# Copies within DRAM from unit 6 on, the gating moved behind a sum, another bank pair: five edits to one attention and MLP kernel

## The chip, the cores and the metric

The kernel runs on one core of one Trainium2 chip. The metric is device time in microseconds (us) of one execution; a kernel's time is the median of several. The profile comes from one profiled execution. The engines are PE (TensorE: matmuls, with PEld for its weight loads), DVE (VectorE), ACT (ScalarE), POOL (GpSimd) and SP (SyncE), which here only issues DMAs.

## The reference

One block of a transformer with modulated layer norms: attention over the last 512 keys of a cache, then a gated MLP, both added to x. All is fp32.

```python
W = min(4096, max(256, Sk // 4))                       # 512 of 2048 keys
q = (x @ wq).reshape(B, Sq, 32, 128)
scores = einsum("bhqd,bhkd->bhqk", q, k) * 128 ** -0.5 # 16 kv heads for 32 heads
o = softmax(scores) @ v
x = x + ga * (o @ wo)                                  # h = layernorm(x) * (1 + ca) + sa went in
gate = h @ W_gate; up = h @ W_up                       # h = layernorm(x) * (1 + cb) + sb
x = x + gb * (relu(gate) * up) @ W_down
```

x has 2048 rows of 576, the MLP is 4608 wide.

## The kernel before

**Precision.** Every matmul operand is split into hi + lo, two numbers of PE's rounded fp32 type, and a product is hi\*hi + lo\*hi + hi\*lo. ACT casts to hi, POOL subtracts to get lo.

**Attention** runs in 128 units u, each one head against 512 queries. A unit issues on PE: 12 matmuls of scores (L454 to L456), 14 of the next unit's q (L382), 2 that spread the maxima (qm, L482), 12 of the last unit's o (pv, L556 to L558, in two halves `pv_half`), and two pieces of 12 that multiply o by wo and go into acc (L583). Most units subtract the maximum on DVE (L529); the first four and the last let PE subtract it (L525, from mr). POOL makes the lo parts (L538) and part of the sums (L547).

**Steps.** A table of steps (time, function) puts everything else between these: time t = 10 u + k means unit u, slot k. On PE, DVE, ACT and POOL the written order is the order that runs. SP is not under that rule: the framework orders its DMAs by what they wait for and when they come up, so a step's time is only one input to its place there. SP issues one DMA after another, in its order; a load whose buffer isn't free holds up all behind it.

**Loads.** wq (L188, rwA), kv (L202, rkv) and wo (L217, roga) come in per head, each into one of two raw buffers, are gated (wo only, L221 on DVE) and split. `wm` (L136) are loads of the modulation, `wa_P` and `wb_P` (L844) those of early MLP weights.

**Copies within DRAM.** wg and wu are laid out anew in DRAM, in `wlay` (and `wlay0` for the first two tiles), by 152 DMAs from SP (`lay_steps`, issued at L1196). 20 of them fill wlay0. 68 are blocks of shape 2 x 128 x 256 (256 KB), and 64 are strips of 8 or 9 x 32 x 128. The MLP's first half and the steps `w_later` (from t = 546) read the result.

**MLP.** 36 steps m, in two halves over the rows; each makes seven products P1, P6, P2, P7, P5, P4, P3 (a Strassen-like scheme, `prod`, L928, gu), in two halves of 7 matmuls. A product's result takes a pair of PSUM banks from the list `free`, two pairs tagged s, and a third pair tagged x that opens when attention's last tiles of the pool psM are done. P2 and P3 go on in the pairs of P1 and P5. Between a product's halves come `sums` (weights of the scheme, DVE, L734, tiles wr and ws), `others` (loads, splits), and one piece of the down projection of m - 1 (`md_piece`): 12 matmuls (L583) into one bank pair, of which there is one, and the sum into acc on DVE (L594). The second product has two such pieces, one before and one behind its second half. Behind the second half, `evac` reads the product (L949 to L953, L975, L978). `mextra` holds functions for a given product; those marked `sums` are the gating of wd (rogb, L221; in the second and the fourth product of an m) and the statistics of the second layer norm (`ln_half`, at the end of m = 1, 3, 5 and 7). After m = 18 wd and the split weights come back from DRAM, without gating.

**Between the two**, steps h0 prepare the MLP's first inputs: `h0_comb` on DVE (L797), `h0_hi` on ACT, `h0_cut` (L817, L819). In the list below H is 1070; the third number is a step's offset.

Of the kernel before, what the change touches and what calls it, by code (L numbers as in the profile page):

```python
# [21 lines left out]
NFT = F // P  # L22
# [11 lines left out]
def kernel(  # L34
# [13 lines left out]
    nc = tc.nc  # L48
# [211 lines left out]
    def flush(q=None):  # L260
        q = pend if q is None else q
        while q:
            q.pop()()
# [143 lines left out]
    NU = HKV * NQB * 2  # L407
# [10 lines left out]
    def unit(u):  # L418
        return UNITS[u]
# [21 lines left out]
    st_, t4, t5, pt, hi_, lo_, bc, rb, rinv, ks_, pvps, done, o, bps = ({} for _ in range(14))  # L441
# [107 lines left out]
    def pv_half(u, h):  # L549
        g, qb, hd = unit(u)  # L550
        if h == 0:
            pvps[u] = psM.tile([P, 512], F32, tag="mm", name=f"pv{u}")
        ps, v, a, b = pvps[u], vs[g], hi_[u, h], lo_[u, h]
        for j in range(2):
            kt = 2 * h + j
            nc.tensor.matmul(ps, v[:, kt, :], a[:, j, :], start=(kt == 0), stop=False)  # L556
            nc.tensor.matmul(ps, v[:, 4 + kt, :], a[:, j, :], start=False, stop=False)  # L557
            nc.tensor.matmul(ps, v[:, kt, :], b[:, j, :], start=False, stop=(kt == 3))  # L558
        if h:
            done[u] = pvps.pop(u)  # L560
# [91 lines left out]
    def order(m):  # L652
        return ("P1", "P6", "P2", "P7", "P5", "P4", "P3")
# [16 lines left out]
    def lay_steps():  # L670
        def tiles(f):
            return [(wlay[f:f + 2, j, :, xx, 0:256], src[f:f + 2, :, 256 * j:256 * j + 256])
                    for xx, src in enumerate((wg, wu)) for j in range(2)]

        def rest(f, g):
            return [(wlay[f:g, j, 32 * r:32 * r + 32, xx, 256:384], src[f:g, 32 * j:32 * j + 32, 512:640])
                    for xx, src in enumerate((wg, wu)) for j in range(2) for r in range(4)]

        def first(s):
            return [(wlay0[:, j, :, xx, 0:256] if w is None else wlay0[:, j, 32 * r:32 * r + 32, xx, 256:384],  # L680
                     a[0:2, :, 256 * j:256 * j + 256] if w is None else a[0:2, 32 * j:32 * j + 32, 512:640])
                    for xx, a in enumerate((wg, wu)) for j in range(2) for w, r in s]

        return (first([(None, 0)] + [(1, r) for r in range(4)]),
                [s for f in range(2, NFT, 2) for s in tiles(f)] +
                [s for f in (2, 10, 19, 28) for s in rest(f, {2: 10, 10: 19, 19: 28, 28: 36}[f])])
# [232 lines left out]
    def prod(m, s, n, xx):  # L919

        hs, w = hop[m // NFP, OPS[s][1]], wop[n]
        ps = pair[m, s][:, xx, :]
        ops = []
        for t in range(2):
            ops += [(w[:, xx, t, :], hs[t]), (w[:, xx, 3 + t, :], hs[t]), (w[:, xx, t, :], hs[3 + t])]
        ops.append((w[0:96, xx, 2, :], hs[2][0:96]))
        for i, (a, c) in enumerate(ops):
            nc.tensor.matmul(ps, a, c, start=s not in ("P2", "P3") and i == 0, stop=i == len(ops) - 1,  # L928
                             skip_group_check=True)
# [27 lines left out]
    npair, px, free, kind = [0], {}, ["s", "s"], {}  # L957
# [71 lines left out]
    def step(name, t, fn, *args):  # L1029
        sched.append((t + PLAN.get(name, 0), len(sched), fn, args))  # L1030
# [161 lines left out]

    step("T.ohi2", e, o_hi, NU - 2)
    step("T.olo2", e, o_lo, NU - 2)
    for i, ab in enumerate(sum(lay_steps(), [])):
        step("lay", 400 + 3.5 * i, lambda ab=ab: nc.sync.dma_start(*ab))  # L1196
    mextra = {}

    def mat(m, s, fn, sums=False):
# [12 lines left out]
    for i in range(4):  # L1212
        m = 2 + 2 * i
# [10 lines left out]
    def sums(m, i):  # L1224

        for k, s in {1: [(0, "S1")], 2: [(0, "S4")], 5: [(1, "S3")], 6: [(1, "S2")]}.get(i, []):
            if 0 < m + k < NFP:
                w_sums(m + k, s)
        for fn in mextra.pop((m, i - 1, True), []):
            fn()  # L1230

    def others(m, i):
        w_prep(7 * m + i + 2)
# [6 lines left out]
    def mlp_slots():  # L1240
        for m in range(NB):
            md = [lambda k=k, qt=qt: md_piece(m - 1, k, qt) for k in range(2) for qt in range(4)] if m else []
            for i, s in enumerate(order(m)):
                flush_stores()
                if s not in ("P2", "P3"):
                    new_pair(m, s)
                else:
                    pair[m, s], kind[m, s] = (x[m, {"P2": "P1", "P3": "P5"}[s]] for x in (pair, kind))
                prod(m, s, 7 * m + i, 0)
                if m or i:  # L1250
                    sums(m, i)
                    others(m, i)
                if m and i:
                    md.pop(0)()
                elif filler and not m:
                    filler.pop(0)()
                prod(m, s, 7 * m + i, 1)
                wop.pop(7 * m + i)
                if m and i < 2:
                    md.pop(0)()  # L1260
                elif filler and not i:
                    filler.pop(0)()
                evac(m, s)
                if s not in ("P1", "P5"):
                    free.append(kind[m, s])
                yield
        for k in range(2):
            for qt in range(4):
                md_piece(NB - 1, k, qt, (psS, "s") if qt % 2 else None)
        flush_stores()  # L1270
        assert not mextra and not filler
# [10 lines left out]
    def open_x():  # L1282
        psM_scope.__exit__(None, None, None)
        px["x"] = ctx.enter_context(tc.tile_pool(name="psX", bufs=1, space=bass.MemoryType.PSUM,
                                                 reuse_waits="tile"))
        free.insert(0, "x")
        filler.extend([lambda q=q: wo_piece(NU - 1, q)() for q in range(4)])


# [19 lines left out]
    for key, t, at_ in [(("l", 0, 0), 2, 96), (("l", 1, 0), 2, 96), (("l", 1, 1), 2, 122), (("l", 0, 1), 2, 122),  # L1309
# [6 lines left out]
        if key[0] == "l":  # L1316
            step("h0.l", H + at_, h0_load, *key[1:], t)
        elif key in H0_COMB:
            step("h0.a", H + at_, h0_comb, *H0_COMB[key], t)
        else:  # L1320
            step("h0.h", H + at_, h0_hi, key, H0_CUT[key], t)
            step("h0.c", H + at_ + (6 if t == 2 else 4 if at_ // 10 % 2 else 6),
                 then(lambda key=key, t=t: h0_cut(key, H0_CUT[key], t, key == "T2")))
# [38 lines left out]
    for u in range(NU):  # L1362
        run(u, 0)
        if u > 1 and u % 2 == 0:
            o_hi(u - 2)
            o_lo(u - 2)
        s_half(u, 0)
        s_half(u, 1)
        max_pre(u)
        if u:  # L1370
            sum_pre(u - 1)
        run(u, 1)
        if u + 1 < NU:
            qproj(u + 1, 0, 14)
        else:
            piece(at[10 * u + 1])
        run(u, 2)
        spread(u)
        max_bc(u)
        if u + 1 < NU:  # L1380
            q_hi(u + 1)
        run(u, 3)
        if 10 * u + 3 in at:
            piece(at[10 * u + 3])
        if u > 1 and u % 2:
            o_hi(u - 2)
            o_lo(u - 2)
        run(u, 4)
        if u:
            pv_half(u - 1, 0)  # L1390
        flush(pend_act)
        exp_half(u, 0)
        flush()
        run(u, 5)
        exp_half(u, 1)
        if u:
            sum_bc(u - 1)
        if u + 1 < NU:
            q_lo(u + 1)
        ksum_op(u, 0)  # L1400
        ksum_op(u, 1)
        run(u, 6)
        if u:
            pv_half(u - 1, 1)
        if 10 * u + 6 in at:
            piece(at[10 * u + 6])
        run(u, 7)
        if u:
            o_mul(u - 1)
        flush()  # L1410
        run(u, 8)
        hi_half(u, 1)
        flush(pend_act)
        lo_half(u, 0)
        lo_half(u, 1)
        run(u, 9)
# [56 lines left out]
```

## Time and profile before

| | |
|---|---|
| median of 3 runs | 3032.86 us (3030.03 to 3036.67) |
| profiled execution, its own time | 3032.14 us |
| its span, first to last instruction | 3030.4 us |
| mean granted clock of PE | 0.985 |
| first matmul of the MLP (L928) | 1704.62 us from the span's start |
| HBM read and written | 278.17 MB, 172.20 MB |

In the views an instruction stands as: line, engine, operation, out<-in, shapes, count. A row of a timeline ends with the idle time ahead of it and what ended that. The chain of waits goes back from the last instruction to what released each one; shares of it are shares of time on the path that set the end. SPq rows are DMA issues on SP; their length is the time of the issue, not of the transfer.

### The profile page before, as it was taken

Reading aid. Unit: us, or ns where it says so; the run is one execution under the profiler, and the core shown is the slowest. Engines: PE = TensorE matmul, PEld = TensorE weight load, DVE = VectorE, ACT = ScalarE, POOL = GpSimd, SP = SyncE. Lnnn points to the kernel's source line nnn. Section 1 sums busy time; section 2 is a strip of 40 time slices with the busy share of each in tenths; the row PEclk is TensorE's granted clock in tenths of the full one; section 3 lists DMA queues with packets and bytes.
Section 4 is the critical chain, followed back from the end, with each engine's and each line's share of the span. In section 5 each row is a group of like instructions: output and inputs, shape, how many; then the busy total and the mean of one; then the engine's idle time right before and its main releaser. Section 6 shows DMA issues by size and latency. Waiting matters only on the chain.

```text
span 3030.4 us, 41167 instructions
## 1 busy us (share of the span) xinstructions
PE 2901.1 (96%) x15406; PEld 2527.0 (83%) x15406; DVE 2116.5 (70%) x2916; ACT 1365.2 (45%) x1869; POOL 1857.3 (61%) x1308
## 2 busy tenths in 40 slices
PE   6799999999978899999999899999999999999999
PEld 4688888888757788888888788888788888888888
DVE  7888888888746788877889666677777544444444
ACT  4467666676545576666656433333323111111110
POOL 5588888888856788876778666667777211111111
PEclk9899999999989999999999999999999999999999
DMA  4011121112222223322233466667666944444543
GB/s 145 21 50 52 50 72 68 66 55 85 102 81 98 90 92 103 129 103 76 77 117 130 133 232 232 251 252 271 254 253 256 347 161 162 162 162 170 177 157 115
DMA packets 167304, 424.75 MB, mean 140 GB/s; under 512 B 15425, under 2 KB 62273, under 8 KB 167105
## 3 DMA queue, kind: packets, MB, share of 16 engines
q1 hardware_dynamic: 131472, 291.58, 29.1%
q10 hardware_dynamic: 35632, 130.53, 10.8%
q8 instruction: 122, 2.00, 0.3%
q14 instruction: 78, 0.63, 0.1%
HBM read 278.17 MB, written 172.20 MB: 149 GB/s over the span
## 4 chain that ended last, share of the span: by engine, by line
PE 83%; DVE 7%; DMA 4%; POOL 2%; issue 2%; ACT 2%; SPq 0%; ACTq 0%; POOLq 0%; DVEq 0%
PE gu L928 25%; PE md L583 14%; PE wo L583 12%; PE qps L382 11%; PE s L455 3%; PE s L456 3%; PE s L454 3%; PE pv L558 3%; PE pv L557 3%; PE pv L556 3%; DVE wr L734 1%; DMA roga<-wo 1%; DMA rkv<-kv 1%; PE qm L482 1%; DVE rogb L221 1%
## 5 line engine op out<-in xcount | busy, mean ns | idle before, releaser
L538 POOL TENSOR_TENSOR lo<-p,hi 128x1024 fp32r<-128x1024 f32 x256 | 610.1, 2404 | 0.9 <-DVE t L474 0.9
L547 POOL TENSOR_TENSOR ks<-ks,p 128x512 f32<-128x512 f32 x256 | 342.6, 1338 | 284.9 <-ACT p L531 218.0
L594 DVE TENSOR_TENSOR acc<-md,acc 128x576 f32<-128x576 f32 x288 | 217.5, 755 | 394.3 <-PE md L583 393.8
L583 PE MATMUL md<-wogb,hhi 128*128 128x288 f32 x2304 | 472.4, 297 | 17.8 <-DVE acc L594 17.8
L583 PEld LDWEIGHTS md<-wogb,hhi 128*128 128x128 f32 x2304 | 384.9, 189 | 46.6 <-DVE acc L594 26.3
L459 DVE TRANSPOSE_TENSOR_REDUCE t<-s 128x32 f32<-128x1024 f32 x256 | 316.5, 1243 | 138.0 <-PE s L456 126.8
L928 PE MATMUL gu<-hop_B,wop 128*128 128x512 f32 (+1 forms) x1512 | 372.5, 393 | 0.0
L583 PE MATMUL md<-wogb,hlo 128*128 128x288 f32 x1152 | 340.9, 296 | 0.0
L382 PE MATMUL qps<-hTa,wA 128*128 128x512 f32 x1288 | 314.8, 396 | 21.5 <-DVE rb L564 11.7
L944 POOL TENSOR_TENSOR hlo<-r,hhi 128x512 fp32r<-128x512 f32 x72 | 94.2, 1309 | 382.9 <-issue 240.9
L583 PE MATMUL wo<-woga,ohi 128*128 128x288 f32 x1472 | 313.3, 306 | 16.1 <-ACT wo L616 14.5
L928 PEld LDWEIGHTS gu<-hop_B,wop 128*128 128x128 f32 (+1 forms) x1512 | 279.7, 189 | 54.6 <-ACT lflh L913 0.4
L928 PE MATMUL gu<-hop_T,wop 128*128 128x512 f32 (+1 forms) x1260 | 313.2, 392 | 3.0 <-DVE rb L564 3.0
L382 PEld LDWEIGHTS qps<-hTa,wA 128*128 128x128 f32 x1288 | 246.4, 192 | 74.7 <-DVE rb L564 12.2
L529 DVE TENSOR_TENSOR p<-s,mb 128x1024 f32<-128x1024 f32 x246 | 290.7, 1219 | 13.0 <-POOL lo L538 8.8
L518 ACT CAST hi<-p 128x1024 fp32r<-128x1024 f32 x256 | 269.0, 1051 | 7.1
L928 PEld LDWEIGHTS gu<-hop_T,wop 128*128 128x128 f32 (+1 forms) x1260 | 231.2, 188 | 46.6 <-DVE rb L564 3.1
L583 PEld LDWEIGHTS wo<-woga,ohi 128*128 128x128 f32 x1472 | 244.4, 193 | 24.9 <-ACT wo L616 15.9
L531 ACT ACTIVATE p<-p 128x1024 f32<-128x1024 f32 x246 | 259.8, 1056 | 8.0 <-DVE p L529 7.9
L943 ACT CAST hhi<-r 128x512 fp32r<-128x512 f32 x72 | 44.7, 621 | 462.0 <-DVE r L953 458.7
L434 ACT ACTIVATE qhi<-qps 128x512 fp32r<-128x512 f32 x128 | 76.5, 597 | 325.8 <-PE qps L382 325.8
L583 PE MATMUL wo<-woga,olo 128*128 128x288 f32 x736 | 220.7, 300 | 0.1
(205 smaller groups left out, 6308.0 us busy)
## 6 DMA issues: line engine op xcount, KB each, us to landing
wop<-wk_P SPq DMA_DIRECT2D x133, 640.0 KB
wk_P<-wop ACTq DMA_DIRECT2D x119, 640.0 KB
wr<-wlay SPq DMA_DIRECT2D x68, 384.0 KB
dk<-wogb ACTq DMA_DIRECT2D x36, 576.0 KB
wogb<-dk SPq DMA_DIRECT2D x36, 576.0 KB
againq<-akq SPq DMA_DIRECT2D x18, 640.0 KB
rogb<-wd SPq DMA_DIRECT2D x36, 288.0 KB
rwA<-wq SPq DMA_DIRECT2D x32, 320.0 KB
```

The lines of the kernel that those rows point to most:

```text
L382: return [lambda i=i, a=a, b=b: nc.tensor.matmul(ps, a, b, start=(i == 0), stop=(i == n - 1)) for i, (a, b) in enumerate(ops)]
L454: nc.tensor.matmul(ps, k[:, kt, :], qhi[u], start=True, stop=False)
L459: nc.vector.tensor_reduce(t4[u][:, 2 * h:2 * h + 2, :].rearrange("p k b -> p (k b)"), t.rearrange("p k (b j) -> p (k b) j", j=32), axis=AX ...
L518: nc.scalar.copy(hi_[u, h], pt[u, h])
L529: nc.vector.tensor_tensor(p, t, bc[u][:, None, :].to_broadcast([P, 2, 512]), op=ALU.subtract)
L531: nc.scalar.activation(p, p, AF.Exp, bias=0.0, scale=1.0)
L538: nc.gpsimd.tensor_sub(lo_[u, h], pt[u, h], hi_[u, h].bitcast(F32))
L547: nc.gpsimd.tensor_tensor(ks_[u], ks_[u], p[:, j, :], op=ALU.add)
L583: nc.tensor.matmul(ps[:, half, :H2], a[:, sl], w[b][:, cs], start=(n == 0 and seed is None), stop=(n == 5), skip_group_check=seed is not None)
L594: nc.vector.tensor_tensor(av, ps[:, :, :H2], av, op=ALU.add)
L928: nc.tensor.matmul(ps, a, c, start=s not in ("P2", "P3") and i == 0, stop=i == len(ops) - 1, skip_group_check=True)
L944: nc.gpsimd.tensor_sub(lo, r, hi.bitcast(F32))
```

## The change

```diff
-    for i, ab in enumerate(sum(lay_steps(), [])):
-        step("lay", 400 + 3.5 * i, lambda ab=ab: nc.sync.dma_start(*ab))
+    lay0, lay = lay_steps()
+    for i, ab in enumerate(lay0 + lay):
+        n = i - len(lay0) - 2 * NFT + 4
+        step("lay", 60 + 4 * i if i < len(lay0) else 612 + 4 * n if n >= 0 else 140 + 7 * (i - len(lay0)),
+             lambda ab=ab: nc.sync.dma_start(*ab))
...
             if 0 < m + k < NFP:
                 w_sums(m + k, s)
-        for fn in mextra.pop((m, i - 1, True), []):
-            fn()
...
                     md.pop(0)()
                 elif filler and not m:
                     filler.pop(0)()
+                for fn in mextra.pop((m, i - 1, True), []):
+                    fn()
                 prod(m, s, 7 * m + i, 1)
...
-        free.insert(0, "x")
+        free.append("x")
...
-                        ("t2", 1, 158), ("t3", 2, 158), ("T2", 1, 162), ("T3", 2, 162), ("t1", 0, 168),
-                        ("t4", 0, 168), ("t2", 2, 178), ("t1", 1, 178), ("T2", 2, 182), ("t4", 1, 178),
+                        ("t2", 1, 158), ("t3", 2, 154), ("T2", 1, 162), ("T3", 2, 162), ("t1", 0, 158),
+                        ("t4", 0, 168), ("t1", 1, 168), ("t2", 2, 178), ("T2", 2, 182), ("t4", 1, 178),
...
         if u:
             pv_half(u - 1, 0)
+        if u + 1 == NU:
+            pv_half(u - 1, 1)
...
-        if u:
+        if 0 < u < NU - 1:
             pv_half(u - 1, 1)
```

**Copies.** The steps of all 152 copies ran from 400 to 928, one per 3.5. Now the 20 of wlay0 have 60 to 136, one per 4; the 68 blocks 140 to 609, one per 7; the 64 strips 612 to 864, one per 4. On SP, the same stretch between two loads of wo (roga), with a load of wq, one of wlay0 and one of kv between them, before:

```order
L217 DMA roga_7709<-wo 128x576
L1196 DMA wlay<-wu 2x128x256
L188 DMA rwA_7777<-wq 128x640
L844 DMA wa_P_1_7781<-wlay_329 128x384
L1196 DMA wlay<-wu 2x128x256
L1196 DMA wlay<-wg 2x128x256
L202 DMA rkv_1_7844<-kv 128x512
L1196 DMA wlay<-wg 2x128x256
L1196 DMA wlay<-wu 2x128x256 x2
L217 DMA roga_7971<-wo 128x576
```

and now:

```order
L217 DMA roga_7743<-wo 128x576
L1199 DMA wlay<-wg 2x128x256
L188 DMA rwA_7811<-wq 128x640
L844 DMA wa_P_1_7815<-wlay_329 128x384
L1199 DMA wlay<-wg 2x128x256
L202 DMA rkv_1_7877<-kv 128x512
L1199 DMA wlay<-wu 2x128x256
L217 DMA roga_8002<-wo 128x576
```

Six blocks stood there, three do now; the other three stand further ahead. The loads keep their order among themselves but for a few late in attention.

**Gating.** The functions marked `sums` run behind the product's first md piece instead of ahead of it. On DVE, the start of an MLP step, from the sum of the first product's piece (acc_125) to that of the third product's piece (acc_128), before:

```order
L594 TENSOR_TENSOR acc_125<-md_0_0_20629,acc_125 128x576
L734 TENSOR_TENSOR wr_00_20438<-ws_11_20569,wr_00_20438 128x768
L221 TENSOR_TENSOR rogb_20575<-rogb_20575,mrow_14027 128x576
L594 TENSOR_TENSOR acc_126<-md_0_1_20665,acc_126 128x576
L594 TENSOR_TENSOR acc_127<-md_0_2_20686,acc_127 128x576
L975 TENSOR_TENSOR q_20643<-gu_20646,q_20643 128x1024
L734 TENSOR_TENSOR wr_01_20530<-wr_01_20530,ws_11_20569 128x768
L594 TENSOR_TENSOR acc_128<-md_0_3_20724,acc_128 128x576
```

and now:

```order
L594 TENSOR_TENSOR acc_125<-md_0_0_20629,acc_125 128x576
L734 TENSOR_TENSOR wr_00_20437<-ws_11_20569,wr_00_20437 128x768
L594 TENSOR_TENSOR acc_126<-md_0_1_20664,acc_126 128x576
L221 TENSOR_TENSOR rogb_20575<-rogb_20575,mrow_14027 128x576
L594 TENSOR_TENSOR acc_127<-md_0_2_20686,acc_127 128x576
L975 TENSOR_TENSOR q_20643<-gu_20646,q_20643 128x1024
L734 TENSOR_TENSOR wr_01_20530<-wr_01_20530,ws_11_20569 128x768
L594 TENSOR_TENSOR acc_128<-md_0_3_20724,acc_128 128x576
```

The gate (L221) and the sum of the second product's first piece (acc_126) have changed places; all else stands where it stood. The gate of the fourth product and the statistics of the layer norm move behind one sum in the same way; on POOL the latter's four small operations move behind a weight's split.

**Bank pair.** The pair x is put at the end of `free` instead of its front, so the first MLP step's fourth product (P7) takes an s pair, the fifth the other s pair, and the sixth x.

**Second half of pv.** In the last unit the second half of the unit before's pv comes right behind the first. On PE (pv, and the subtraction of the maxima from the scores s), before:

```order
L556 MATMUL pv_16841<-hi_0_16735,againv_16392 128x512
L557 MATMUL pv_16841<-hi_0_16735,againv_16392 128x512
L558 MATMUL pv_16841<-lo_0_16785,againv_16392 128x512
L525 MATMUL s_0_16789<-mr_16835,minus 128x512 x2
L525 MATMUL s_1_16798<-mr_16835,minus 128x512 x2
L556 MATMUL pv_16841<-hi_1_16780,againv_16392 128x512
L557 MATMUL pv_16841<-hi_1_16780,againv_16392 128x512
L558 MATMUL pv_16841<-lo_1_16787,againv_16392 128x512
```

and now:

```order
L558 MATMUL pv_16841<-lo_0_16785,againv_16393 128x512
L556 MATMUL pv_16841<-hi_1_16780,againv_16393 128x512
L557 MATMUL pv_16841<-hi_1_16780,againv_16393 128x512
L558 MATMUL pv_16841<-lo_1_16787,againv_16393 128x512
L556 MATMUL pv_16841<-hi_1_16780,againv_16393 128x512
L557 MATMUL pv_16841<-hi_1_16780,againv_16393 128x512
L558 MATMUL pv_16841<-lo_1_16787,againv_16393 128x512
L525 MATMUL s_0_16789<-mr_16835,minus 128x512 x2
L525 MATMUL s_1_16798<-mr_16835,minus 128x512 x2
```

Six matmuls have moved ahead of the four that subtract.

**h0 steps.** On DVE one sum of unit 122 moves ahead of the subtraction of the maxima in that unit, and two others move one unit earlier each, from the ends of units 123 and 124 to those of 122 and 123.

## The prediction

> **What bounds the kernel now.** I read the page first (busy shares, slices, chain), then a table of stretches, then the chain of waits inside the bad stretches, then SP's timeline there.
>
> ```profile
> PE 2901.1 (96%) x15406; PEld 2527.0 (83%) x15406; DVE 2116.5 (70%) x2916; ACT 1365.2 (45%) x1869; POOL 1857.3 (61%) x1308
> PE   6799999999978899999999899999999999999999
> PEclk9899999999989999999999999999999999999999
> ```
>
> PE is the bound: 96% busy. The rest sits in a few slices: the first two, slices 11 to 14, and some thin loss that tenths hide. Stretches show how much (columns: us, busy us and count of PE, PEld, DVE, ACT, POOL, granted clock, DMA share, GB/s):
>
> ```profile
> 250.00:750.00 500.00, 498.49 (x2648) 434.33 (x2647) 412.58 (x607) 340.10 (x456) 419.05 (x251) 1.00 0.20 66
> 783.40:1020.40 237.00, 189.27 (x897) 161.42 (x896) 141.41 (x201) 117.54 (x161) 151.78 (x100) 0.89 0.27 94
> 1020.40:1300.00 279.60, 279.47 (x1480) 243.50 (x1479) 226.83 (x333) 188.35 (x254) 244.22 (x157) 1.00 0.33 108
> 1997.72:2341.71 343.99, 326.36 (x1758) 283.25 (x1757) 257.82 (x251) 112.90 (x161) 255.50 (x223) 0.99 0.71 258
> 2341.71:2376.99 35.28, 35.28 (x196) 31.23 (x195) 20.74 (x25) 9.97 (x14) 19.72 (x19) 1.00 0.91 323
> ```
>
> Count matmuls, not busy time, because a slow clock hides in busy time. Attention runs 2648 matmuls in 500 us, 5.30 per us. The 897 of the second row would take 169.4 us at that pace; they took 237.0. **The hole costs 67.6 us**, idle and clock (0.89) together. The MLP's clean pace is 196 in 35.28 us, 5.56 per us; the 1758 of the fourth row would take 316.4 us and took 344.0, so 27.6 us are lost there.
>
> **The hole.** Its chain, in order of time (start, us, what):
>
> ```profile
> 784.07 14.20 DMA roga<-wo
> 837.23 11.08 DMA rkv<-kv
> 848.47 12.32 DMA rwA<-wq
> 889.91 11.56 DMA roga<-wo
> 976.63 12.94 DMA rkv<-kv
> ```
>
> Weight loads are late. SP's own timeline, a quiet row and a piece of the hole, and the copies by stretch (783 to 1013, then one half of those from 1013 to 1290; ns shortest/median/longest):
>
> ```profile
> 649.70 0.59 SPq L1196 DMA_DIRECT2D wlay<-wu  x1
> 842.38 5.98 SPq L1196 DMA_DIRECT2D wlay<-wg  x2
> 848.47 6.09 SPq L188 DMA_DIRECT2D rwA<-wq  x1
> ...
> L1196 SPq DMA_DIRECT2D wlay<-wu x19: 582/5342/6973, 778.6 to 1002.3; - x19
> L1196 SPq DMA_DIRECT2D wlay<-wg x19: 583/740/6097, 791.5 to 1007.6; - x19
> ...
> L1196 SPq DMA_DIRECT2D wlay<-wu x32: 631/705/782, 1028.0 to 1271.8; - x32
> ```
>
> An issue takes 0.59 us when the queue has room and up to 6 us in the hole, so SP stands behind a full queue. In the hole 38 copies went through in 230 us: **6.05 us each, loads between them included**, with the 16 DMA engines only 27% busy. So something narrower than the engines' sum is full, and these copies, whose outermost dimension is 2, fill it. The strips after 1013 (outermost dimension 8 or 9) go at 0.7 us an issue, and PE loses nothing beside them (third stretch).
>
> [...]
>
> **The change, part by part.**
>
> *Copies.* A unit has 64 matmuls (12 scores, 14 q, 12 pv, 24 wo, 2 qm), so 12.08 us at the clean pace. Before, a copy's step is 3.5 tenths of a unit, 4.23 us; now 7 tenths, 8.46 us. At 6.05 us of service the old steps overrun by 1.82 us per copy, and 38 of them make 69 us: the hole to within 2 us. The new steps leave 2.4 us of slack per copy, so the queue drains before the next. The order above says the same: between the same two loads stood six copies, now three. What is new is that copies run beside every load from unit 14 to 61. A tight load is this one (SP issues two loads from 685.63; DVE uses the first):
>
> ```profile
> 685.63 7.57 SPq L217 DMA_DIRECT2D roga<-wo  x2
> 693.92 1.52 DVE L221 TENSOR_TENSOR roga<-roga,mrow 128x576 f32<-128x576 f32 x1
> ```
>
> 8.29 us from issue to use, with DVE not waiting. One copy (6.05 us) ahead of such a load leaves 2.2 us; two copies make it late. In the new order one copy mostly stands ahead of a load, two ahead of three roga loads. I expect those copies mostly drained before the load's buffer is free, and take 0.6 us of loss: **67 us gained**, bounds 50 (the rival with pairs) and 67.6. The strips move from units 71 to 92 to units 61 to 86 and cost nothing, as the third stretch shows.
>
> *Gating.* One m of the MLP on DVE, the PE row between; the chain by line over 1960 to 2345 us, and its three longest gates; all gates (ns shortest/median/longest); the page's group of md matmuls:
>
> ```profile
> 2116.80 0.76 DVE L594 TENSOR_TENSOR acc<-md,acc 128x576 f32<-128x576 f32 x1 [2.61 <-PE md L583]
> 2117.48 2.81 DVE L734 TENSOR_TENSOR wr<-ws,wr 128x768 f32<-128x768 f32 x1
> 2120.21 3.74 DVE L221 TENSOR_TENSOR rogb<-rogb,mrow 128x576 f32<-128x576 f32 x1
> 2123.88 0.74 DVE L594 TENSOR_TENSOR acc<-md,acc 128x576 f32<-128x576 f32 x1
> 2126.57 0.76 DVE L594 TENSOR_TENSOR acc<-md,acc 128x576 f32<-128x576 f32 x1 [1.95 <-PE md L583]
> 2124.67 0.53 PE L583 MATMUL md<-wogb,hhi 128*128 128x288 f32 x2 [3.11 <-DVE acc L594]
> ...
> by line: PE gu L928 42.6%; PE md L583 27.2%; DVE wr L734 10.9%; DVE rogb L221 6.5%; issue 3.1%; DVE acc L594 2.4%; DMA hx_T<-hb 1.5%; DMA hk_T<-hy_T 1.3%; DVE q L975 0.9%; POOL hlo L944 0.8%; POOL wop L706 0.6%; POOL wop L705 0.4%; POOL wog
> ...
> 2120.29 3.67 DVE rogb L221
> 2235.27 3.69 DVE rogb L221
> 2274.88 3.69 DVE rogb L221
> ...
> L221 DVE TENSOR_TENSOR rogb<-rogb,mrow x36: 745/752/3765, 1718.7 to 2360.7; 128x576 f32<-128x576 f32 x36
> ...
> L583 PE MATMUL md<-wogb,hhi 128*128 128x288 f32 x2304 | 472.4, 297 | 17.8 <-DVE acc L594 17.8
> ```
>
> The second product has two md pieces and one bank for them, so the second piece waits for the first one's sum, which stood behind sums and gate. Here PE idles 3.11 us of a 3.74 us gate. Gates make 6.5% of 385 us on the chain, 25 us; PE's own idle for the sum is 17.8 us in all, so that caps the gain. With the gate behind the sum, PE starts the second piece at 2121; its sum then waits for the gate and ends at 2125.4, while PE, after 1.7 us of md and 1.6 us of the next product's half, wants that sum at 2124.3: 1.1 us come back as a new wait. This holds for the three gates of 3.7 us; shorter ones, by the same sum, hide up to 2.6 us. 17.8 less 3.3 given back, and less 1.5 us that I leave to waits of which L734 is the cause: **13 us gained**, bounds 3 (the first rival) and 17.8. The gate of the fourth product moves behind its sum too, into a piece of DVE idle; the statistics of m 1, 3, 5, 7 likewise: nothing.
>
> *Bank pair.* The first MLP's fourth product took the pair x, which is free only after the last unit's o; it now takes an s pair, evacuated by L975 long before (rows: PE's two halves of that product, with a wo piece between them; the casts that this piece needs; then, for the next part, PE and ACT further ahead, and a pair of h0 sums on the chain):
>
> ```profile
> 1725.92 2.17 PE L928 MATMUL gu<-hop_T,wop 128*128 128x512 f32 x7 [3.01 <-DVE rb L564]
> 1730.77 1.80 PE L928 MATMUL gu<-hop_T,wop 128*128 128x512 f32 x7
> 1725.98 0.62 ACT L568 CAST ohi<-rb 128x512 fp32r<-128x512 f32 x1 [1.04 <-DVE rb L564]
> 1726.67 1.29 POOL L572 TENSOR_TENSOR olo<-rb,ohi 128x512 fp32r<-128x512 f32 x1 [0.40 <-ACT ohi L568]
> 1706.93 0.53 PE L583 MATMUL wo<-againo,ohi 128*128 128x288 f32 x2 [0.54 <-ACT acc L592]
> 1706.25 0.63 ACT L592 COPY acc<-wo 128x576 f32<-128x576 f32 x1
> ...
> 1651.93 3.39 DVE lfb L797 x2
> ```
>
> The 3.01 us go, but the wo piece needs olo, ready at 1726.67 + 1.29 = 1727.96, for its last 7 of 12 matmuls, so the second half starts near 1729 where it started at 1730.77: **2 us gained**, bounds 0 and 3.
>
> *The second pv half and the h0 steps.* PE has the pv half done while it waits for the maxima, but the wo piece behind starts at 1706.93 on ACT's copy, itself behind two exponentials: 0, bounds 0 and 1.4 gained. The h0 sums cost DVE 3.39 us a pair, and a pair at a unit's end costs PE a wait; there are two such unit ends before and two after, each one unit earlier: 0, bounds 3.4 lost and 3.4 gained (one pair more or less in the way). On SP one weight load passes one load of h in the MLP: nothing, since neither is on the chain.
>
> *Sum.* The profiled execution took 3032.1 us (span 3030.4 and 1.7 around it), 0.7 us under the median of 3032.9. 67 + 13 + 2 = 82: **2950 us**.
>
> **Rivals.**
> - *The gate keeps its price* (2961). A gate takes 0.75 us in most m and 3.74 us here while POOL works, so its length hangs on what POOL does then; moved by one sum it may meet longer work, and push the second sum and the sums of L734 by as much. For: L734 holds 10.9% of this chain. Against: PE then has two more pieces to hide it. The gain shrinks to 2 to 3 us. [...]
> - *Pairs of copies* (2968). The three roga loads behind two copies land late, as in the hole: 14.20 us against 8.29 allowed, 5.9 us each, 18 us. Against: with 2.4 us of slack per copy the older one should be gone.
> [...]
> - *The copies were not the cause, or don't move in time* (3017). SP is not ordered by hand, a step is only its hint; the order shows them moved. Then 15 us remain.
>
> **How the numbers follow.** Forecast 0.68, gate 0.12, pairs 0.10, not the cause 0.04, slower 0.03, no change 0.01, better than all bounds 0.02. The range 2940 to 2970 takes in the bounds of gating, pair and small edits around the forecast, and both first rivals: some 0.88. Faster by over 0.2% (6 us, about what can be told from no change): 0.96; within it 0.01; slower 0.03.
>
> **What would show it.** In the profile after: no chain rows of 11 us loads, SP issues at 0.6 us throughout, granted clock 1.00 in slices 11 to 14, and the MLP some 68 us earlier. L221 leaves the chain between the two sums; PE's idle for L594 falls from 17.8 to about 5 us. The wait on L564 before the fourth product is gone, a shorter one on olo in its place. The forecast is wrong if roga loads show landings over 8 us with DVE waiting, or if L734 takes over what L221 leaves.

## The result and the profile after

The changed kernel takes **2951.93 us** (median of 4 runs, 2950.61 to 2953.43), the kernel before 3034.36 us (3030.03 to 3036.67): ratio 0.973, 95% interval 0.9713 to 0.9747. Predicted were 2950 us, between 2940 and 2970. The profiled execution took 2953.43 us (span 2951.6).

The page of the changed kernel, its busy line and two rows of slices:

```profile
PE 2880.4 (98%) x15406; PEld 2514.9 (85%) x15406; DVE 2116.3 (72%) x2916; ACT 1365.7 (46%) x1869; POOL 1864.6 (63%) x1308
PE   6799999999999999999999999999999999999999
PEclk9899999999999999999999999999999999999999
```

The dent of slices 11 to 14 is gone, in PE and in its clock. Two stretches of attention, the first of them one of the prediction's, both with copies running now (us, busy us and count of PE, PEld, DVE, ACT, POOL, clock, DMA share, GB/s):

```profile
250.00:750.00 500.00, 498.49 (x2648) 434.57 (x2647) 412.63 (x607) 340.09 (x457) 419.04 (x251) 1.00 0.25 84
750.00:952.40 202.40, 200.86 (x1060) 174.14 (x1059) 165.84 (x237) 141.64 (x195) 177.26 (x120) 1.00 0.29 95
```

2648 matmuls in 500 us is the clean pace of before, with copies beside it; 1060 in 202.4 us is nearly the same (5.24 per us against 5.30). SP's copies (ns shortest/median/longest, first and last start) from 174 to 783 us, then one half of those from 783 to 1013. Below them DVE's longest waits from 174 to 1290 us, of before (two rows) and of the changed kernel (one row): us in total, times, longest.

```profile
L1199 SPq DMA_DIRECT2D wlay<-wu x41: 567/588/2878, 190.5 to 782.2; - x41
L1199 SPq DMA_DIRECT2D wlay<-wg x32: 578/586/7107, 239.7 to 764.0; - x32
L1199 SPq DMA_DIRECT2D wlay<-wg x26: 587/737/1542, 785.0 to 1001.3; - x26
...
DVE t L459 <- PE s L456: 92.0, 69, 2.6
...
DVE roga L221 <- DMA roga<-wo: 25.5, 4, 12.1
...
DVE t L459 <- PE s L456: 99.8, 78, 2.2
```

The usual issue is 0.59 us again (a few still stand, the longest 7.1 us, and nobody on the path waits for what is behind them). DVE's 25.5 us for roga are gone: it now waits almost only for PE, as it should when PE is the bound. The first MLP matmul starts at 1639.21 us where it started at 1704.62: **65.4 of the 78.8 us by which the span is shorter come from attention, 13.4 from the MLP.**

The MLP: PE's and its weight loads' rows for md on the page, the chain by line over the prediction's stretch of time (1960 to 2345 us), and the longest gap left, on DVE, POOL and PE:

```profile
L583 PE MATMUL md<-wogb,hhi 128*128 128x288 f32 x2304 | 470.8, 297 | 9.3 <-DVE acc L594 9.3
L583 PEld LDWEIGHTS md<-wogb,hhi 128*128 128x128 f32 x2304 | 386.2, 189 | 33.6 <-DVE acc L594 12.5
...
by line: PE gu L928 60.0%; PE md L583 34.8%; DVE wr L734 3.5%; DVE gu L952 0.4%; DVE c L951 0.4%; DVE acc L594 0.4%; issue 0.3%; PE ltlh L910 0.2%; DVEq L734 0.0%; DVE c L953 0.0%
...
2178.87 9.06 DVE L734 TENSOR_TENSOR wr<-wr,wr 128x768 f32<-128x768 f32 x1
2187.86 0.74 DVE L594 TENSOR_TENSOR acc<-md,acc 128x576 f32<-128x576 f32 x1
...
2178.84 1.28 POOL L706 TENSOR_TENSOR wop<-wr,wop 128x512 fp32r<-128x512 f32 x1
2180.10 1.42 POOL L181 TENSOR_TENSOR wogb<-rogb,wogb 128x576 fp32r<-128x576 f32 x1
...
2185.86 1.25 POOL L778 TENSOR_TENSOR hx_T<-hx_T,hy_T 128x512 fp32r<-128x512 f32 x1
...
2188.66 0.85 PE L583 MATMUL md<-wogb,hhi 128*128 128x288 f32 x2 [5.47 <-DVE acc L594]
```

L221 is off the chain here. The same stretch of time holds later work now; over the same work as before (1894.6 to 2279.6 us) L221 has 0.8% of the chain and L734 4.8%, where they had 6.5% and 10.9%. PE's idle for L594 is 9.3 us where it was 17.8. What is left is L734: one sum (S3, the one of slot 5) took 9.06 us, while POOL ran back to back from 2176.89 to 2187.11, and the sum into acc stood behind it. S3 stands right ahead of the late sum into acc in all four waits that make the 9.3 us.

### The profile page after: what moved, and what is told of

Read it like the earlier page. It is cut to its first block, busy times and chain, and to the rows that moved or that the text cites. A ratio compares the mean times of both kernels' runs of the same rounds, so it can differ in the third digit from the quotient of the medians.

```text
span 2951.6 us, 41158 instructions
## 1 busy us (share of the span) xinstructions
PE 2880.4 (98%) x15406; PEld 2514.9 (85%) x15406; DVE 2116.3 (72%) x2916; ACT 1365.7 (46%) x1869; POOL 1864.6 (63%) x1308
## 4 chain that ended last, share of the span: by engine, by line
PE 90%; DVE 5%; POOL 2%; issue 1%; ACT 1%; DMA 0%; ACTq 0%; SPq 0%; DVEq 0%; POOLq 0%
PE gu L928 26%; PE md L583 15%; PE wo L583 13%; PE qps L382 13%; PE s L455 4%; PE s L456 4%; PE s L454 4%; PE pv L558 3%; PE pv L557 3%; PE pv L556 3%; PE qm L482 1%; POOL lo L538 1%; DVE wr L734 1%; DVE t L459 1%; DVE hTa L370 0%
## 5 line engine op out<-in xcount | busy, mean ns | idle before, releaser
L594 DVE TENSOR_TENSOR acc<-md,acc 128x576 f32<-128x576 f32 x288 | 217.8, 756 | 393.5 <-PE md L583 392.4
L583 PE MATMUL md<-wogb,hhi 128*128 128x288 f32 x2304 | 470.8, 297 | 9.3 <-DVE acc L594 9.3
L583 PEld LDWEIGHTS md<-wogb,hhi 128*128 128x128 f32 x2304 | 386.2, 189 | 33.6 <-DVE acc L594 12.5
L928 PE MATMUL gu<-hop_B,wop 128*128 128x512 f32 (+1 forms) x1512 | 371.8, 393 | 0.0
L928 PEld LDWEIGHTS gu<-hop_B,wop 128*128 128x128 f32 (+1 forms) x1512 | 279.0, 189 | 54.5 <-ACT lflh L913 0.9
L928 PE MATMUL gu<-hop_T,wop 128*128 128x512 f32 (+1 forms) x1260 | 313.5, 393 | 0.0
L583 PE MATMUL wo<-woga,ohi 128*128 128x288 f32 x1472 | 306.0, 301 | 1.5 <-DVE lfa L362 1.5
L928 PEld LDWEIGHTS gu<-hop_T,wop 128*128 128x128 f32 (+1 forms) x1260 | 231.9, 189 | 43.3
```

Of the source, the lines that this page charges most:

```text
L583: nc.tensor.matmul(ps[:, half, :H2], a[:, sl], w[b][:, cs], start=(n == 0 and seed is None), stop=(n == 5), skip_group_check=seed is not None)
L594: nc.vector.tensor_tensor(av, ps[:, :, :H2], av, op=ALU.add)
```

## Experiments

**1. The copies alone** (before, with the new steps only).

```diff
-    for i, ab in enumerate(sum(lay_steps(), [])):
-        step("lay", 400 + 3.5 * i, lambda ab=ab: nc.sync.dma_start(*ab))
+    lay0, lay = lay_steps()
+    for i, ab in enumerate(lay0 + lay):
+        n = i - len(lay0) - 2 * NFT + 4
+        step("lay", 60 + 4 * i if i < len(lay0) else 612 + 4 * n if n >= 0 else 140 + 7 * (i - len(lay0)),
+             lambda ab=ab: nc.sync.dma_start(*ab))
```

> The kernel before with the new steps of the copies alone. Theory (the copies overfill their DMA engines at 4.23 us a copy and fit at 8.46 us): the hole of 67.6 us goes, so 66 to 68 us less than before (2966 us against 3033), PE's matmuls from 783 us on at 5.30 per us. Rival (the five edits work only together, or the hole moves): less than 50 us gained, or a hole between units 14 and 61.

Measured: 2967.12 us against 3033.82 (ratio 0.9777, 0.9762 to 0.9792): **66.7 us gained**, and in 250 to 750 us the same 2648 matmuls as the changed kernel. The term of 67 us stands.

**2. The gating alone** (before, with the gate behind the sum).

```diff
-        for fn in mextra.pop((m, i - 1, True), []):
-            fn()
...
+                for fn in mextra.pop((m, i - 1, True), []):
+                    fn()
```

> The kernel before with the functions marked sums moved behind the md piece alone. Theory: 13 us less than before (3020 us), all of it in the MLP's first half; PE's idle for L594 falls from 17.8 us to about 9 us as in the changed kernel. Rival (the gate keeps its price): 3 us or less.

Measured: 3020.78 us (ratio 0.9955, 0.994 to 0.9971): **13.0 us gained**. Its page's rows for md, the first two, and below them that of the weight loads before:

```profile
L583 PE MATMUL md<-wogb,hhi 128*128 128x288 f32 x2304 | 470.8, 297 | 9.4 <-DVE acc L594 9.3
L583 PEld LDWEIGHTS md<-wogb,hhi 128*128 128x128 f32 x2304 | 385.7, 189 | 34.3 <-DVE acc L594 13.0
...
L583 PEld LDWEIGHTS md<-wogb,hhi 128*128 128x128 f32 x2304 | 384.9, 189 | 46.6 <-DVE acc L594 26.3
```

The matmul row lost 8.4 us of idle, the run 13.0; the weight loads' row lost 13.3 (26.3 to 13.0). In a wait the weight load stops before the matmul: in the longest of the changed kernel its row has 5.89 us of idle, the matmul's 5.47. That the weight loads' row holds the whole gain is argued from this agreement, not shown: the matmuls of the row also were busy for 1.6 us less (472.4 to 470.8).

**3. What fills the queue: the form of the copies, or the bytes?** The blocks at their old steps, with both sides' outermost dimension 128 in place of 2; same bytes, same rows of 1 KB.

```diff
-            return [(wlay[f:f + 2, j, :, xx, 0:256], src[f:f + 2, :, 256 * j:256 * j + 256])
+            return [tuple(ap.rearrange("f p n -> p f n") for ap in
+                          (wlay[f:f + 2, j, :, xx, 0:256], src[f:f + 2, :, 256 * j:256 * j + 256]))
```

> The kernel before, its old steps, with the 68 blocks copied as 128 x 2 x 256 in place of 2 x 128 x 256: the same bytes in the same 1 KB runs, with 128 as the outermost dimension. SP's order puts them much closer together, up to 18 between two loads, between units 17 and 27. [...] Rival (bytes to and from DRAM, or the number of copies, are what fills the queue): a hole of at least 60 us, now near 280 to 400 us, and no gain.

Measured: 2974.78 us (ratio 0.9799, 0.9774 to 0.9824), 59 us gained with no copy slowed down. SP's order comes out differently for the new form: up to 18 copies stand between two loads, from 250 us on. SP's issues there, and PE's stretch:

```profile
L1197 SPq DMA_DIRECT2D wlay<-wu x68: 552/640/1504, 249.8 to 733.5; - x68
L1197 SPq DMA_DIRECT2D wlay<-wg x66: 552/644/1491, 257.2 to 684.6; - x66
...
250.00:750.00 500.00, 492.69 (x2603) 429.04 (x2602) 404.44 (x595) 335.33 (x449) 409.75 (x246) 0.99 0.34 106
```

No issue takes over 1.5 us though far more copies run per us (DMA share 0.34, above the 0.27 of the old hole). 45 matmuls fewer than 2648 are 8.5 us: two units took 17.92 and 14.99 us from qm to qm in place of 12.08, where loads stand behind many copies. So bytes and number are not what was full: the outermost dimension decides (longest issue 1.50 us at 128, 6.97 in the old hole at 2). The copies also moved forward in time here; run 4 shows that an early place alone does not help.

**4. Rate or place?** The changed kernel with the blocks at 4 tenths of a unit (4.83 us), early as they now are.

```diff
-        step("lay", 60 + 4 * i if i < len(lay0) else 612 + 4 * n if n >= 0 else 140 + 7 * (i - len(lay0)),
+        step("lay", 60 + 4 * i if i < len(lay0) else 612 + 4 * n if n >= 0 else 140 + 4 * (i - len(lay0)),
```

> The changed kernel with the 68 blocks at one per 4 steps (4.83 us) in place of one per 7, still from step 140. Theory (rate decides): 6.05 less 4.83 is 1.22 us a copy, 68 of them make 83 us, less what the loads' slack of 6 to 8 us takes up: 65 to 85 us over the changed kernel (2952), as a hole between 180 and 600 us with SP issues of 5 us. Rival (the place decides: before, the copies met the parked loads and those of wlay0 late in attention): within 10 us of the changed kernel.

Measured: 3019.17 us (3013.42 to 3025.76), 67 us over the changed kernel. The hole is back at its new place, 174 to 560 us:

```profile
174.00:560.00 386.00, 352.52 (x1789) 304.68 (x1788) 281.50 (x407) 229.84 (x308) 281.01 (x168) 0.96 0.24 79
...
L1199 SPq DMA_DIRECT2D wlay<-wg x28: 578/4309/6997, 239.3 to 557.3; - x28
...
409.81 13.40 DMA roga<-wo
```

1789 matmuls take 337.8 us at the clean pace and took 386. That is 48 of the 67 us; from 560 to 1000 us, where the queue empties at first, 2227 matmuls stand against 2314 in the changed kernel, another 16 us. The rate decides.

**5. How near is the edge?** The same at 5.5 tenths, 6.64 us a copy.

```diff
-        step("lay", 60 + 4 * i if i < len(lay0) else 612 + 4 * n if n >= 0 else 140 + 7 * (i - len(lay0)),
+        step("lay", 60 + 4 * i if i < len(lay0) else 612 + 4 * n if n >= 0 else 140 + 5.5 * (i - len(lay0)),
```

> The changed kernel with the blocks at 5.5 tenths of a unit (6.64 us) instead of 7 (8.46 us). By the service of 6.05 us for each copy a step of 6.64 us leaves 0.6 us of slack, so the queue still drains: within 5 us of the changed kernel, about 2953, with SP's issues at 0.6 us. Rival (pairs of copies): with so little slack the older copy is not gone when the next stands behind it, some tight loads land 6 us late, and the run is 10 to 30 us longer, with chain rows of loads of 11 us. If service is really 6.9 us or more, the hole is back: 68 copies times 0.3 us or more, 20 us and up.

Measured: 2959.43 us (2958.26 to 2961.19), 7.5 us over the changed kernel, so over the 5 us that were allowed. But attention hardly moved; its stretch, then the first 700 us of the MLP of this run and of the changed kernel:

```profile
250.00:750.00 500.00, 498.02 (x2643) 433.27 (x2642) 411.27 (x606) 339.38 (x455) 418.92 (x251) 1.00 0.27 90
...
1639.65:2339.65 700.00, 683.34 (x3727) 598.86 (x3726) 494.46 (x531) 229.59 (x329) 472.39 (x417) 1.00 0.70 257
...
1639.10:2339.10 700.00, 687.09 (x3751) 603.67 (x3750) 490.55 (x534) 230.54 (x331) 473.52 (x418) 0.99 0.71 259
```

The MLP starts 0.55 us later, so the copies keep up: a copy's service is about 6.64 us at most, as 6.05 says. But it is near the edge. SP's issues were expected at 0.6 us; from 170 to 790 us SP's timeline has 35 rows (one or two issues each) of over 4 us, against 6 in the changed kernel, and two roga loads of 13.93 and 14.17 us stand on the chain, as the rival had it, only without its price. The other 5 us of the profiled run's loss lie in an MLP that the edit does not touch (24 matmuls fewer, at 5.56 per us 4.3 us). There PE's weight loads wait 17.0 us for L594, 12.5 in the changed kernel. Why all four runs are longer is open.

**6. The bank pair undone** (the changed kernel, x first again).

```diff
-        free.append("x")
+        free.insert(0, "x")
```

> The changed kernel with its bank pair alone undone: the first MLP's fourth product takes pair x again. The prediction's sum gave the pair 2 us, so by it this run is 2 us longer than the changed kernel. By what its trace shows (from the last unit's qm to the MLP's 21st gu stop 48.97 us in the kernel before, 48.59 us in the changed one) the pair moved the wait and removed nothing: then this run is within 1 us of the changed kernel, and that stretch within 0.5 us of 48.6, with a wait of about 3 us on L564 back and those on olo gone.

Measured: 2953.62 us (ratio 0.9742, 0.9727 to 0.9758), not to be told from 2951.93. PE's rows from the last unit's qm: this run (qm, the product's first half, its second half), then, with the pair, run 8 below (qm, the wo piece's two waits, the second half), then the changed kernel itself (a piece's matmul, the second half):

```profile
1657.76 0.29 PE L482 MATMUL qm<-t,quad 128*128 128x16 f32 x2
1661.06 1.91 PE L928 MATMUL gu<-hop_T,wop 128*128 128x512 f32 x7 [3.01 <-DVE rb L564]
1664.41 1.78 PE L928 MATMUL gu<-hop_T,wop 128*128 128x512 f32 x7
...
1656.55 0.29 PE L482 MATMUL qm<-t,quad 128*128 128x16 f32 x2
1660.59 0.53 PE L583 MATMUL wo<-againo,ohi 128*128 128x288 f32 x2 [1.63 <-ACT ohi L568]
1661.93 0.40 PE L583 MATMUL wo<-againo,olo 128*128 128x288 f32 x1 [0.81 <-POOL olo L572]
1662.97 1.78 PE L928 MATMUL gu<-hop_T,wop 128*128 128x512 f32 x7
...
1663.53 0.68 PE L583 MATMUL wo<-againo,ohi 128*128 128x288 f32 x2
1664.97 2.43 PE L928 MATMUL gu<-hop_T,wop 128*128 128x512 f32 x7
```

Qm to the second half: 6.65 us without the pair, 6.42 with it. **At full clock the pair is worth 0.23 us.** The prediction read 4.85 us between the two halves in the trace of before; here, in the same order, it is 3.35 us. Before's profiled execution had PE at a lower speed in that wo piece (0.68 us for two matmuls that take 0.43 here), 1.5 us that belong to no step. So had the changed kernel's, in a part of the piece, 0.8 us. Over the 22.7 us from the qm on the granted clock is 0.92 in these two, 1.00 in this run and in run 8. That also makes the expected 48.6 us miss: the stretch is 1.2 us shorter here.

**7. The last pv half and the h0 list undone**, each alone.

```diff
-        if u + 1 == NU:
-            pv_half(u - 1, 1)
...
-        if 0 < u < NU - 1:
+        if u:
```

> The changed kernel with the last unit's second pv half put back behind the score steps. The prediction gave this edit 0, at most 1.4 us gained, since the wo piece behind it waits for ACT's copy into acc anyway. Then this run is within 1.5 us of the changed kernel, PE's gap ahead of that wo piece is 1.0 us instead of 1.5, and the stretch from the last unit's qm to the next unit's first wo piece keeps its length.

```diff
-                        ("t2", 1, 158), ("t3", 2, 154), ("T2", 1, 162), ("T3", 2, 162), ("t1", 0, 158),
-                        ("t4", 0, 168), ("t1", 1, 168), ("t2", 2, 178), ("T2", 2, 182), ("t4", 1, 178),
+                        ("t2", 1, 158), ("t3", 2, 158), ("T2", 1, 162), ("T3", 2, 162), ("t1", 0, 168),
+                        ("t4", 0, 168), ("t2", 2, 178), ("t1", 1, 178), ("T2", 2, 182), ("t4", 1, 178),
```

> The changed kernel with the old list of h0 steps alone. The prediction put the change of the list at nothing, between 3.4 us lost and 3.4 us gained. The traces show units 120 to 124 taking 64.06 us before and 64.85 us after, so by them this run is 0.8 us shorter than the changed kernel, and units 122, 123 and 124 take 12.1, 13.9 and 13.8 us again in place of 14.6, 13.9 and 12.1. If the list has nothing to do with it, the three stay at 14.6, 13.9 and 12.1.

Measured: 2953.64 us (2946.06 to 2956.02) and 2952.41 us (2947.86 to 2957.72); neither is told from 2951.93. The last unit, from qm to some 0.2 us before the next, in the run without the pv edit, in the kernel before and in the changed one:

```profile
1629.50:1656.10 26.60, 24.33 (x120) 20.70 (x121) 11.22 (x17) 11.59 (x17) 17.64 (x11) 0.94 0.51 161
...
1696.50:1722.40 25.90, 23.11 (x120) 19.51 (x121) 12.42 (x17) 11.48 (x17) 17.68 (x12) 1.00 0.48 159
...
1631.60:1657.50 25.90, 23.59 (x119) 19.37 (x120) 12.34 (x17) 11.48 (x17) 17.68 (x12) 1.00 0.48 155
```

From qm to qm the unit takes 26.85, 26.13 and 26.11 us: at a clock of 1.00 it is the same length without the pv edit and with it, so the edit is worth 0. The 0.7 us more in the first row go with its clock of 0.94, so that run alone can't price it. With the old h0 list units 122 to 124 take 12.1, 13.9 and 13.8 us, with the new one 14.6, 13.9 and 12.1: the list costs 0.8 us there, below what the runs' times can show.

**8. What is left of the gate's price: a matter of place?** The changed kernel with three of the sums of L734 (slots 1, 2 and 5) behind the md piece too.

```diff
-                    sums(m, i)
+                    if i not in (1, 2, 5):
+                        sums(m, i)
...
+                if i in (1, 2, 5):
+                    sums(m, i)
```

> The changed kernel with the sums of L734 for slots 1, 2 and 5 also put behind the second product's sum into acc. Theory: what is left of the idle time for L594 (9.3 us) is the price of these sums standing ahead of that sum on DVE, long (5 to 9 us instead of 1 to 3) where they meet a row of GpSimd operations. Then L594's idle falls under 3 us, and the time is 6 to 9 us under the changed kernel's, about 2944. Rival: what stretches DVE's work there stretches whatever stands in that place, the sum into acc itself and the sums behind it, which then hold up the next product's evacuations: the idle time moves to L928 and the time is within 2 us of the changed kernel's.

Measured: 2951.77 us (ratio 0.9738, 0.9723 to 0.9754): no gain. L594's idle is 8.7 us in place of 9.3. DVE ahead of the longest gap (2.8 us for the matmul, 3.3 for its weight load):

```profile
2014.13 2.53 DVE L734 TENSOR_TENSOR wr<-ws,wr 128x768 f32<-128x768 f32 x1
2016.59 3.74 DVE L221 TENSOR_TENSOR rogb<-rogb,mrow 128x576 f32<-128x576 f32 x1
2020.26 0.74 DVE L594 TENSOR_TENSOR acc<-md,acc 128x576 f32<-128x576 f32 x1
```

The rival has the time and the reason right: what now stands there, a sum and the gate, is stretched in turn, and the second sum into acc is late. The place it has wrong, since the idle stays with L594 and L928 waits only 1.9 us. One execution can't tell 8.7 from 9.3: with this part of the code as in the changed kernel, runs 5 and 6 have 12.4 and 5.1 us.

**9. Or of the engine?** S3 on GpSimd, then S3 and S4 (in these, and in run 10, L734 and L928 of the changed kernel are L735 and L929).

```diff
-        nc.vector.tensor_tensor(flat(out), flat(a), flat(b), op=op)
+        eng = nc.gpsimd if s == "S3" else nc.vector
+        eng.tensor_tensor(flat(out), flat(a), flat(b), op=op)
```

and for the second `s in ("S3", "S4")`.

> The changed kernel with one of the four sums of L734 (S3, the one that stands ahead of a late sum into acc in all four remaining gaps: 1.92, 1.87, 1.33 and 5.89 us) given to GpSimd instead of VectorE. Theory: VectorE's operation on two SBUF tiles waits there while GpSimd runs operations back to back; on GpSimd itself the sum takes its turn, an estimated 1.9 us (512 columns take 1.29), and the sum into acc no longer waits. PE's idle for L594 falls from 9.3 us to 2 us or less, and the time is 6 to 11 us under the changed kernel's, about 2943. Rival: GpSimd, busy 368 of 500 us here, then casts the MLP's weight tiles late; PE's idle turns up as waits on L705 and L706 and the time is within 3 us of the changed kernel's.

> As the last, with S4 on GpSimd too. S4 stands ahead of none of the four gaps. Theory: no further gain, within 2 us of the run with S3 alone, since what is left of VectorE's waits is not on PE's path. Rival (whatever stands on VectorE next to a GpSimd run pays, S4 among it): another 2 to 4 us less. If GpSimd is the bound by then, this run is longer than the one with S3 alone, with PE waiting on L705 or L706.

Measured: 2951.62 us (ratio 0.973, 0.971 to 0.9749) and 2965.86 us (0.9775, 0.9756 to 0.9795). PE's waits from 1700 to 2400 us, changed kernel, S3 moved, S3 and S4 moved (total, times, longest), and two rows of POOL with S3 moved:

```profile
PE md L583 <- DVE acc L594: 9.3, 4, 5.5
...
PE gu L929 <- POOL wop L706: 5.3, 5, 2.6
PE gu L929 <- DMA wop<-wk_P: 1.3, 2, 0.7
PE md L583 <- DVE acc L594: 0.6, 2, 0.3
...
PE md L583 <- DVE acc L594: 9.5, 5, 2.9
PE gu L929 <- POOL wop L706: 4.5, 8, 1.0
...
2181.15 1.82 POOL L735 TENSOR_TENSOR wr<-wr,wr 128x768 f32<-128x768 f32 x1
2183.62 1.97 POOL L706 TENSOR_TENSOR wop<-wr,wop 128x512 fp32r<-128x512 f32 x1
```

The theory is right about L594 (0.6 us left) and wrong about the time: PE waits for POOL's casts instead, the rival's result. With S4 there as well 14 us are lost; PE's waits above are 14.0 us in place of 9.3, so most of that loss is not explained by them and stays open.

**10. Less work.** S3 left out, so that the MLP's weights lack it and the result is another.

```diff
-        nc.vector.tensor_tensor(flat(out), flat(a), flat(b), op=op)
+        if s != "S3":
+            nc.vector.tensor_tensor(flat(out), flat(a), flat(b), op=op)
```

> The changed kernel with the sum S3 of L734 left out (13 or so operations of 128x768 on two SBUF tiles; the MLP's weights then lack it). Moving S3 within VectorE and giving it to GpSimd left the time where it was, PE's idle only changed its name. [...] Rival: only places matter; then the price moves to the next sum or gate in line, the idle stays at 10 us or more, and the time is within 3 us of the changed kernel's.

Measured: 2948.28 us (ratio 0.9723, 0.9703 to 0.9743), 3.7 us under the changed kernel, just over the rival's 3. The rival's idle of 10 us or more did not come: PE's waits from 1700 to 2400 us fall from 9.3 to 5.1 us, L594's part of them to 3.3 us. DVE's other sums from 1800 to 2300 us, one of them before (changed kernel) and now:

```profile
L734 DVE TENSOR_TENSOR ws<-wr,wr 128x768 f32<-128x768 f32 x13 | 15.8, 1214 | 0.0
...
L735 DVE TENSOR_TENSOR ws<-wr,wr 128x768 f32<-128x768 f32 x13 | 28.1, 2164 | 0.0
```

S3 had 43.0 us of DVE there; its neighbour S2 took 12.3 of them over, the other sums and the gates 8.5. So part of the price is work and part is passed on. No version tried beats the changed kernel while computing the same by more than its runs scatter.

## Why the prediction was right

- *What bounds the kernel, and the hole.* Right in size, and in mechanism as far as the runs reach. 67 us predicted, 66.7 measured alone (run 1). Its cause, that copies with an outermost dimension of 2 fill something narrow, is shown by run 3; that the rate decides, by run 4; that a copy's service is about 6.64 us at most, by run 5. That the copies were not the cause, a rival at 3017 us, fell with run 1. What the narrow thing is, is not shown: the trace has no row of which of the 16 engines a copy used, and the 27% in the hole is a mean over all 16.
- *The rivals on copies.* The three roga loads behind two copies cost nothing that DVE's waits show: pairs of copies did not decide at 8.46 us. For the copies to use up all gains, the slower case, each would have to take 9.7 us (8.46 and 82 us over 68 copies); it is 6.64 at most.
- *Gating.* The mechanism is right: the gate stood between the two sums, and moving it gave 13.0 us (run 2) of 13 predicted. The working of the size is not, and that it met the 13 is luck. PE's idle in the matmuls' row was to fall from 17.8 to about 5 us and fell to 9.3: L734 kept not 1.5 us but all of what is left, while the 3.3 us that were to come back as new waits behind the gate are not among PE's four waits. By this row the gain would have been 8.4 us. The run gained 4.6 more, which the row never held, so 17.8 us was no sure cap; the weight loads' row (26.3 less 13.0, 13.3) comes near to the whole.
- *"The gate of the fourth product moves into a piece of DVE idle: nothing."* This is not shown. In the changed kernel such gates met POOL's run (3.38 us at 1845.16, 3.35 us at 1919.10). No wait of PE ends on them, but the chains of two of the four waits, to 1858.78 and 1932.67, go back through S3 and a weight's cast to just these two. The first rival, the gate keeping its price, fell; its reason, that the length hangs on what POOL does then, holds for what stands in the gate's place (S3: 9.06 us beside POOL's row).
- *Bank pair.* Mis-sized: 2 us predicted, 0.23 measured at full clock (run 6). The mechanism is as told, the wait on L564 gone and shorter ones on ohi and olo in its place; the failing step is the second half's start of 1730.77 us, which was read from a piece that ran at a lowered clock (0.92 over the 22.7 us there). Of the clock, the prediction looked at long stretches only, not at this one.
- *The pv half and the h0 steps.* 0 for the first; 0.8 us lost for the second, inside its bounds.
- *Sum.* 66.7 and 13.0 measured alone make 79.7 of the 82.4 us between the medians; the small edits add some −0.6 by the traces. The 3 us between are no more than scatter: sets of runs of the kernel before have medians of 3034.36 and 3031.2 us. So that 2950 was met to within 2 us is luck in part, too.

## What to carry to other kernels

Here the queue's price came out as its service time (6.05 us a copy) against the interval at which copies were put in (4.23 us): look for both (issues of 6 us in place of 0.6 led to the service). Slowing the copies to one per 8.46 us removed the whole loss (66.7 us), and an outermost dimension of 128 most of it (59 us). For a wait on TensorE, read the weight loads' row as well as the matmuls': here the first lost 13.3 us of idle, the second 8.4, the run 13.0 us. A duration taken from one place in one execution is compared with the same instruction elsewhere: two matmuls of the wo piece took 0.68 us in one execution and 0.43 in another, and the 1.5 us that this makes over the piece looked like a step's. Where two engines seem to get in each other's way, as DVE and POOL here, a move of one instruction has to be tried: the gate's gave 13.0 us, three more moves of sums gave nothing or lost 14 us, and leaving a sum out gave 3.7.

## What the runs showed of the hardware

- In the changed kernel a DVE sum of two SBUF tiles (S3) took 0.95 us from 1745.11 on, where POOL idled till 1745.92, and 9.06 us from 2178.87 on, while POOL ran seven operations of 0.7 to 1.4 us without a pause; it ended 0.8 us after the last of them. So it was stretched over a whole row of POOL's operations, not over one. By what means is not shown. POOL's operations aren't of one length either: in run 9, with S3 moved, one L706 took 1.97 us in place of 1.28; what DVE did beside it is not shown.
- The same matmuls ran at a lowered clock in some executions and not in others, behind waits of the same length. Over some 22.7 us from the last unit's qm on, the granted clock was 0.92 in the kernel before and 1.00 in run 6, both with the wait of 3.01 us on L564; it was 0.92 in the changed kernel and 1.00 in run 8, both with the two waits of 1.63 and 0.81 us. The cost in the wo piece was 1.5 us before and 0.8 us in the changed kernel. What sets the clock is not shown.
- The MLP's length differs between executions with the same code there: the profiled ones of the changed kernel, of run 5 and of both runs 7 (pv, then h0) have 1312.4, 1317.3, 1315.0 and 1313.5 us from the first MLP matmul to the end. The waits of PE's weight loads for L594 go with it: 12.5, 17.0, 15.9 and 14.1 us, at other sums each time. That this is how DVE and POOL happen to meet is the author's estimate, not shown.
